# Packing the last quad's first-half operands four and five steps earlier in a four-layer attention and Fourier kernel

## The chip, the cores and the metric

The kernel runs on one core of one Trainium2 chip. The metric is the device time of one execution in microseconds (us). Three timed runs of the kernel before gave 2179.58, 2181.9 and 2183.06 us; the median is 2181.9 us. The trace comes from a fourth, profiled execution, which took 2185.11 us and whose span from the first to the last instruction is 2183.4 us. A core has five engines with an instruction queue each: PE (matrix multiply; PEld is its weight load), DVE, ACT and POOL (vector and scalar work), and SP, which in this kernel does nothing but issue DMAs, one after the other.

## The reference

Four layers alternate: sliding-window attention, Fourier mixing, attention, Fourier mixing, each on a layer-normalised input and added to it. The change touches the attention layers alone (layers 0 and 2 of the four, called the first and the second attention layer here).

```python
B, S, D = 1, 2048, 640
def _A_ref(x, wqkv, wo):
    H = 32; Dh = D // H; W = 256
    q, k, v = split_heads(x @ wqkv)              # 32 heads of 20 columns
    scores = einsum("bhqd,bhkd->bhqk", q, k) * Dh ** -0.5
    mask = (i - j >= 0) & (i - j < W)            # a window of 256 keys
    p = softmax(where(mask, scores, -1e9))
    return merge_heads(p @ v) @ wo
x = x + _A_ref(_layernorm(x), A_wqkv, A_wo)
x = x + _B_ref(_layernorm(x), ...)               # Re(DFT_seq(DFT_hidden(x)))
x = x + _A_ref(_layernorm(x), A_wqkv, A_wo)
x = x + _B_ref(_layernorm(x), ...)
```

## The kernel before

Every float32 product is made from two reduced-precision parts of each operand (three matmuls). In an attention layer the 32 heads are worked in eight quads of four heads, numbered 0 to 7, and the 2048 rows in sixteen blocks of 128. `heads` runs one loop over `step`, 16 steps to a quad. In one step it does three things for three different places of this order:

- `s_head` (L631, L636), ten steps ahead (`LEAD = 10`): the scores of one query block, only to find each row's maximum. PE multiplies `qp` by `kp`, DVE adds the mask and takes the maximum into `mc`. The first query block of a quad has 128 key columns, the second 256, the others 384. Quad 7's first block is done in step 102.
- `t_pair` and `t_exp` (L659, L669), in the step itself: the transposed scores with the maximum subtracted, which costs an extra row of `qp` (61 rows instead of 60), and the exponential on ACT, masked on POOL (L675, L679). Quad 6 is in steps 96 to 111.
- `pv` (L694, L701), one step behind: probabilities times values.

The extra row of `qp` is made by `m_rows` every fourth step: PE transposes `mc` (L644), ACT copies it to `mt` (L647), and SP stores it into `qp` with two small DMAs (L649, `qp<-mt` in the profile). The rows of quad 6's third quarter of the sequence are stored in step 98, and the first `t_pair` that reads them is that of step 102.

`kp` and `qp` are two tiles each, for even and odd quads. They are filled by `pack(quad, j)`, which loads one quarter `j` of the sequence (512 columns) from the projections that were stored in DRAM as `qk_d`. It makes twelve DMAs (L594) of 80 KB: three for each of four groups, first `kp` for the two heads pairs, then `qp`. The loop issues one group a step over four steps. When a pack begins is fixed by the list `due`: each entry holds the value of `s = step + 10` from which the pack of quad `q`, quarter `j` is made, the number of projection rounds that must be done by then, `q` and `j`. The projection matmuls (L257, `project`, `pieces`) are spread over the steps as filling between the attention matmuls; `nf` is the number of rounds for a step, the largest of a pace that ends the projection at step 96 (`ROWS_AT`) and of the paces that the entries of `due` ask for. From step 96 on the filling is instead the first part of the output projection (`partials`, also L257, and its addition on DVE, L978), whose inputs SP loads then: the residual rows (L952, 320 KB each), the attention outputs and their scales (L859, L865, 256 KB each).

All DMAs of a layer go through SP in the order of the program. The other engines' instructions are in an order of their own, fixed when the program is written out; an engine waits only where its next instruction lacks data or a free buffer.

Of the kernel before, what the change touches and what calls it, by code (L numbers as in the profile page):

```python
# [21 lines left out]
NQ = H // 4  # L22
# [8 lines left out]
AHEAD = 8  # L31
EARLY = 3
AHEAD_X = 4
AFTER = 4
ROWS_AT = 96
FIRST = 7
LATE = 9
BACK = 2
# [26 lines left out]
class Net:  # L65
# [540 lines left out]
    def heads(self, xsrc, xdst, hook):  # L606
# [98 lines left out]
        def finish(quad, bk):  # L705
# [10 lines left out]
            def store():  # L716
# [6 lines left out]
        total = NCH * NSB * per_piece  # L723
        done = [2 * NSB * per_piece]

        due = [(16 * q + 4 * j - AHEAD + 2 * (q == NQ - 1),
                ((-(-160 * (q + 1) // P) - 1) * NSB + 2 * (j // 2) + 2) * per_piece, q, j)
               for q in range(1, NQ) for j in range(NSB)]
        self.xsrc = xsrc
# [47 lines left out]
        for step in range(-LEAD, steps + 1):  # L777
# [11 lines left out]
            if due and s >= due[0][0]:  # L789
                while done[0] < due[0][1]:  # L790
                    fill(15)
                q, j = due.pop(0)[2:]
# [6 lines left out]
            if done[0] < total:  # L799
                nf = max([FIRST if t < -2 else (total - done[0]) / max(1, ROWS_AT - t)]  # L800
                         + [(d - done[0]) / max(1, at - s) for at, d, _, _ in due])
# [1064 lines left out]
```

## Time and profile before

| | us |
|---|---|
| timed runs | 2179.58, 2181.9, 2183.06 |
| median of the timed runs | 2181.9 |
| profiled execution | 2185.11 |
| its span | 2183.4 |
| PE busy in it | 2119.3 (97%) |
| DVE busy | 1602.8 (73%) |
| ACT busy | 1139.6 (52%) |
| POOL busy | 961.1 (44%) |
| DMA, mean over the span | 182 GB/s |

The profile is read as follows. A row of the timeline has the start (us from the span's start), the length in us, the engine, the line of the kernel, the operation, the tiles written and read, the shape and the number of merged instructions; in square brackets stands the idle time of the engine before the row and what ended it. "SPq" rows are issues of DMAs, and their length is the time that SP took to issue, not the transfer. The steps that the change touches lie near 412 to 446 us and 1498 to 1535 us.

### The profile page before, as it was taken

The page shows a single profiled execution, that of the slowest core. Times are in us where ns is not written, and L with a number is a line of the kernel's source. Part 1 is how long each engine was busy: PE and PEld are TensorE (multiplying, and loading weights), DVE is VectorE, ACT ScalarE, POOL GpSimd, SP SyncE. Part 2 cuts the span into 40 slices and gives each one's busy share as a digit, 9 for nine tenths or more (in the row PEclk, how much of TensorE's full clock was granted, in tenths as well). Part 3 has the DMA queues.
Part 4 walks back from the last instruction along what each step waited for, and adds up shares of the span by engine and source line. Part 5 has one row for each costly group of instructions (what it writes and reads, how often), then busy time and mean ns, then how long its engine had stood idle before and what let it go on. Part 6 is the DMA issues. An engine that isn't in the chain of part 4 may idle for free.

```text
span 2183.4 us, 48970 instructions
## 1 busy us (share of the span) xinstructions
PE 2119.3 (97%) x17872; PEld 1785.2 (82%) x17872; DVE 1602.8 (73%) x3931; ACT 1139.6 (52%) x2125; POOL 961.1 (44%) x1562
## 2 busy tenths in 40 slices
PE   8999999988999999999999999999899999999999
PEld 7987777777778888889999877776778888888899
DVE  6358888876897868786661588888768968677666
ACT  3117777756554545552441277777565645445332
POOL 3037777755513223232330377768555033231324
PEclk9999999999999999999999999999999999999999
DMA  5546666775565454655645566667845453545643
GB/s 185 174 159 193 197 189 206 214 229 178 182 197 185 133 186 135 212 194 193 209 152 182 163 188 194 193 207 216 215 155 182 142 186 126 175 157 204 220 165 125
DMA packets 227089, 398.40 MB, mean 182 GB/s; under 512 B 39969, under 2 KB 86561, under 8 KB 226849
## 3 DMA queue, kind: packets, MB, share of 16 engines
q1 hardware_dynamic: 226848, 395.28, 57.0%
q8 instruction: 141, 2.31, 0.4%
q14 instruction: 100, 0.81, 0.1%
HBM read 273.94 MB, written 120.06 MB: 180 GB/s over the span
## 4 chain that ended last, share of the span: by engine, by line
PE 79%; DVE 7%; DMA 5%; ACT 4%; issue 3%; POOL 2%; SPq 1%; ACTq 0%; DVEq 0%; POOLq 0%
PE banks L1416 29%; PE banks L239 14%; PE banks L257 13%; PE banks L694 7%; PE banks L659 6%; PE banks L631 5%; PE banks L1704 5%; DVE banks L636 1%; DMA kp<-qk_d 1%; DMA kp<-u_d 1%; DVE qp L232 1%; ACT pt L669 1%; PE banks L341 1%; ACT big L1039 1%; POOL rs L1087 1%
## 5 line engine op out<-in xcount | busy, mean ns | idle before, releaser
L636 DVE CUSTOM_DVE_ANT_0 banks<-banks,mask 128x384 f32<-128x384 f32 (+2 forms) x1024 | 527.0, 556 | 116.7 <-PE banks L631 98.9
L669 ACT ACTIVATE pt<-banks 128x768 f32<-128x768 f32 (+2 forms) x512 | 393.4, 771 | 170.7 <-PE banks L659 78.0
L675 POOL TENSOR_SCALAR_AFFINE_SELECT pt<-pt 128x256 f32<-128x256 f32 x512 | 219.0, 428 | 212.6 <-ACT pt L669 190.9
L257 PE MATMUL banks<-big,wc 64*128 64x512 f32 x1920 | 272.4, 394 | 0.4 <-DVE pt L442 0.4
L659 PE MATMUL banks<-qp,kp 61*128 61x384 f32 (+2 forms) x1024 | 210.1, 380 | 21.5 <-DVE mc L636 16.4
L694 PE MATMUL banks<-pt,vq 128*32 128x128 f32 x5760 | 211.9, 278 | 3.5 <-ACT pt L669 3.5
L631 PE MATMUL banks<-kp,qp 60*128 60x384 f32 (+2 forms) x1024 | 210.2, 350 | 4.9 <-DMA qp<-qk_d 3.5
L257 PEld LDWEIGHTS banks<-big,wc 64*128 64x128 f32 x1920 | 186.3, 185 | 23.0 <-DVE pt L442 0.5
L226 ACT ACTIVATE qp<-pt 128x512 fp32r<-128x512 f32 (+1 forms) x200 | 123.2, 625 | 129.0 <-DVE pt L1347 52.1
L679 POOL TENSOR_SCALAR_AFFINE_SELECT pt<-pt 128x256 f32<-128x256 f32 x448 | 188.3, 420 | 0.0
L232 DVE TENSOR_TENSOR qp<-pt,qp 128x512 fp32r<-128x512 f32 (+1 forms) x198 | 157.8, 805 | 40.2 <-ACT qp L226 38.6
L694 PEld LDWEIGHTS banks<-pt,vq 128*32 128x32 f32 x5760 | 142.7, 110 | 51.8 <-issue 36.3
L659 PEld LDWEIGHTS banks<-qp,kp 61*128 61x128 f32 x1024 | 108.4, 185 | 85.3 <-DVE mc L636 62.3
L1416 PE MATMUL banks<-qp,big 128*128 128x512 f32 x648 | 153.5, 390 | 0.0
L631 PEld LDWEIGHTS banks<-kp,qp 60*128 60x128 f32 x1024 | 126.7, 186 | 29.6 <-DVE mc L636 16.0
L1345 POOL TENSOR_TENSOR pt<-pt,pt 128x512 f32<-128x512 f32 x32 | 47.3, 1478 | 232.2 <-DMA pt<-c 140.3
L226 ACT ACTIVATE c<-pt 128x512 fp32r<-128x512 f32 x146 | 90.3, 625 | 109.0 <-POOL pt L1325 56.1
L636 DVE DVE_READ_ACCUMULATOR2_ANT mc<- 128x1 f32 x1024 | 143.6, 140 | 0.0
L1416 PEld LDWEIGHTS banks<-qp,big 128*128 128x128 f32 x648 | 120.7, 188 | 25.0 <-POOL qp L232 0.9
L232 DVE TENSOR_TENSOR c<-pt,c 128x512 fp32r<-128x512 f32 x144 | 113.5, 791 | 26.3 <-ACT c L226 24.0
L1416 PE MATMUL banks<-qp,xc 128*128 128x512 f32 x480 | 117.9, 393 | 3.4 <-DVE xc L232 1.9
L552 POOL CAST c<-x 128x512 fp32r<-128x512 f32 x64 | 38.8, 610 | 166.5 <-ACT x L544 162.3
(253 smaller groups left out, 4482.4 us busy)
## 6 DMA issues: line engine op xcount, KB each, us to landing
pt<-c SPq DMA_DIRECT2D x166, 512.0 KB
qk_d<-c SPq DMA_DIRECT2D x80, 512.0 KB
kp<-qk_d SPq DMA_DIRECT2D x384, 80.0 KB
qp<-qk_d SPq DMA_DIRECT2D x384, 80.0 KB
kp<-u_d SPq DMA_DIRECT2D x32, 640.0 KB
o_d<-ou SPq DMA_DIRECT2D x64, 256.0 KB
x_d<-x SPq DMA_DIRECT2D x48, 320.0 KB
v_d<-pt SPq DMA_DIRECT2D x16, 768.0 KB
```

The source lines that it names most:

```text
L226: nc.scalar.activation(hi, src, AF.Copy, scale=-1.0 if neg else 1.0)
L232: (eng or nc.vector).tensor_tensor(out=lo, in0=src, in1=hi.bitcast(F32), op=OP.subtract)
L239: self.nc.tensor.matmul(p, x, y, start=n == 0, stop=n == last)
L257: self.nc.tensor.matmul(ps[a], x[r], y[r], start=half + i == 0, stop=half == 1 and i == n - 1, skip_group_check=True)
L631: nc.tensor.matmul(p, qp[quad % 2][b:b + 60, z, qb * P:(qb + 1) * P], kp[quad % 2][b:b + 60, z, k0 * P:(qb + 1) * P], start=True, stop=True)
L636: nc.vector.tensor_tensor_reduce(out=p, in0=p, in1=self.mask[:, 384 - n * P:], scale=1.0, scalar=NEG, op0=OP.add, op1=OP.max, accum_out=mc ...
L659: nc.tensor.matmul(self.banks[:, banks[e], :n * P], kp[quad % 2][b:b + 61, z, kb * P:(kb + 1) * P], qp[quad % 2][b:b + 61, z, kb * P:(kb + ...
L669: nc.scalar.activation(pt[quad, kb][:, 2 * z:2 * z + 2, :n * P], self.banks[:, b0:b1 + 1, :n * P], AF.Exp, scale=SCALE)
L675: nc.gpsimd.affine_select(out=t[:, :, 0:P], in_=t[:, :, 0:P], pattern=[[0, 2], [1, P]], compare_op=OP.is_ge, fill=0.0, base=0, channel_mul ...
L679: nc.gpsimd.affine_select(out=t[:, :, 256:384], in_=t[:, :, 256:384], pattern=[[0, 2], [-1, P]], compare_op=OP.is_gt, fill=0.0, base=0, ch ...
L694: nc.tensor.matmul(self.banks[32 * h:32 * h + 32, bank, :P], vq[:, 96 * (kb % 4) + 21 * h:96 * (kb % 4) + 21 * h + 32], t[:, h, (qb - kb) ...
L1416: nc.tensor.matmul(self.banks[:, bk, :], p, b[q], start=start and m == 0, stop=stop and last and m == 2, skip_group_check=True)
```

## The change

The start values of the last quad's four packs become a list. For quad 7 the old expression gives `s` = 106, 110, 114, 118 for the four quarters, which is step 96, 100, 104, 108. The new list gives 102, 105, 114, 118, which is step 92, 95, 104, 108. Nothing else is changed; the number of DMAs and their contents are the same.

```diff
 ROWS_AT = 96
+LAST_DUE = (-10, -7, 2, 6)
 FIRST = 7
...
-        due = [(16 * q + 4 * j - AHEAD + 2 * (q == NQ - 1),
+        due = [(16 * q + (4 * j - AHEAD if q < NQ - 1 else LAST_DUE[j]),
                 ((-(-160 * (q + 1) // P) - 1) * NSB + 2 * (j // 2) + 2) * per_piece, q, j)
                for q in range(1, NQ) for j in range(NSB)]
```

The order of the three L594 groups by step, with the pack of quad 6's last quarter written 6.3 and so on:

| step | before | after |
|---|---|---|
| 90, 91 | 6.3 | 6.3 |
| 92, 93 | 6.3 | 6.3 and 7.0 |
| 94 | none | 7.0 |
| 95 | none | 7.0 and 7.1 |
| 96, 97, 98 | 7.0 | 7.1 |
| 99 | 7.0 | none |
| 100 to 103 | 7.1 | none |
| 104 to 111 | 7.2, 7.3 | 7.2, 7.3 |

## The prediction

> **What bounds the kernel now.** I read the page first, then PE's timeline for the end of the heads in both attention layers, then the granted clock there, then SP's timeline, since the change reorders only DMAs.
>
> ```profile
> PE 2119.3 (97%) x17872; PEld 1785.2 (82%) x17872; DVE 1602.8 (73%) x3931; ACT 1139.6 (52%) x2125; POOL 961.1 (44%) x1562
> PE 79%; DVE 7%; DMA 5%; ACT 4%; issue 3%; POOL 2%; SPq 1%; ACTq 0%; DVEq 0%; POOLq 0%
> ```
>
> PE is busy for 97% of the span and carries 79% of the chain that ended last: time lost on PE is time lost. The 5% that the chain gives to DMA is where the change can act. PE's timeline, second layer then first:
>
> ```profile
> 1499.10 0.86 PE L257 MATMUL banks<-big,wc 64*128 64x512 f32 x6
> ...
> 1506.95 0.44 PE L659 MATMUL banks<-qp,kp 61*128 61x384 f32 x2
> ...
> 1525.23 0.86 PE L694 MATMUL banks<-pt,vq 128*32 128x128 f32 x24
> 1527.24 0.45 PE L659 MATMUL banks<-qp,kp 61*128 61x384 f32 x2 [1.14 <-DMA qp<-mt]
> 1527.49 0.28 PE L631 MATMUL banks<-kp,qp 60*128 60x128 f32 x1
> 1529.66 0.32 PE L631 MATMUL banks<-kp,qp 60*128 60x128 f32 x1 [1.90 <-DMA qp<-qk_d]
> ...
> 1541.69 0.45 PE L659 MATMUL banks<-qp,kp 61*128 61x384 f32 x2 [1.40 <-DVE mc L636]
> ```
>
> ```profile
> 439.99 0.44 PE L659 MATMUL banks<-qp,kp 61*128 61x384 f32 x2 [1.22 <-DMA qp<-mt]
> ...
> 442.14 0.47 PE L631 MATMUL banks<-kp,qp 60*128 60x128 f32 x1 [1.61 <-DMA qp<-qk_d]
> ```
>
> The L631 rows with 128 columns are a quad's first query block, so this is step 102, and 1506.95 is step 96 (the first t_pair with 384 columns after quad 5's short blocks). In step 102 PE waits twice in each layer: first its L659 for the row maxima of quad 6 (`qp<-mt`, 1.22 and 1.14 us), then the second L631 for the last group of pack 7.0 (1.61 and 1.90 us). Only the second wait is for something that the change issues earlier. The clock around it:
>
> ```profile
> 442.00:445.00 3.00, 2.86 (x21) 2.86 (x23) 0.36 (x2) 0.00 (x0) 0.94 (x2) 0.50 0.78 267
> 445.00:448.00 3.00, 3.00 (x50) 2.46 (x49) 2.21 (x9) 2.21 (x5) 1.47 (x3) 0.93 0.69 213
> ...
> 1504.00:1507.00 3.00, 3.00 (x64) 2.11 (x52) 2.57 (x11) 1.92 (x7) 2.46 (x5) 1.00 0.49 160
> 1507.00:1510.00 3.00, 2.62 (x38) 1.52 (x36) 2.80 (x10) 2.35 (x6) 2.01 (x5) 1.00 0.51 128
> ...
> 1516.00:1519.00 3.00, 2.67 (x46) 2.15 (x38) 2.43 (x11) 1.56 (x5) 1.69 (x5) 1.00 1.07 270
> ...
> 1528.00:1531.00 3.00, 1.34 (x17) 1.34 (x19) 0.52 (x4) 0.59 (x1) 1.46 (x3) 0.97 0.88 268
> 1531.00:1534.00 3.00, 3.00 (x36) 2.11 (x35) 1.34 (x5) 0.90 (x2) 1.03 (x3) 0.50 0.86 208
> 1534.00:1537.00 3.00, 2.94 (x50) 2.49 (x50) 1.96 (x9) 2.35 (x5) 1.75 (x4) 0.96 0.86 212
> ```
>
> The last three columns are clock, DMA share and GB/s. Behind the waits the granted clock is 0.50 for 3 us, which costs 3 x 0.50 = 1.5 us; the edges (0.93; 0.97 and 0.96) add 0.2 us in each layer. So the pair of waits costs 1.7 us more than it shows. The DMA engines are half idle in steps 95 to 97 (0.49, 0.51) and full in step 98 to 99 (1.07). Filling that hole is what speaks for the change. What speaks against it is SP:
>
> ```profile
> 1492.18 1.19 SPq L524 DMA_DIRECT2D qk_d<-c  x1
> ...
> 1497.45 1.18 SPq L594 DMA_DIRECT2D kp<-qk_d  x3
> 1498.68 3.08 SPq L594 DMA_DIRECT2D qp<-qk_d  x3
> 1501.86 0.35 SPq L621 DMA_DIRECT2D vq<-v_d  x1
> 1502.26 1.63 SPq L594 DMA_DIRECT2D qp<-qk_d  x3
> 1503.98 0.61 SPq L711 DMA_DIRECT2D sm<-ou  x1
> 1504.64 0.48 SPq L712 DMA_DIRECT2D o_d<-ou  x1
> 1505.22 0.37 SPq L717 DMA_DIRECT2D r_d<-rc  x1
> 1505.69 1.09 SPq L649 DMA_DIRECT2D qp<-mt  x2
> 1506.84 1.19 SPq L594 DMA_DIRECT2D kp<-qk_d  x3
> 1508.13 0.35 SPq L621 DMA_DIRECT2D vq<-v_d  x1
> 1508.58 0.83 SPq L952 DMA_DIRECT2D big<-x_d  x2
> 1509.46 1.11 SPq L594 DMA_DIRECT2D kp<-qk_d  x3
> ...
> 1522.67 1.53 SPq L649 DMA_DIRECT2D qp<-mt  x2
> 1524.25 1.22 SPq L594 DMA_DIRECT2D qp<-qk_d  x3
> ```
>
> From 1497.45 to 1510.57 every row begins within 0.10 us of the end of the one before: SP is never idle there, although the DMA engines are. It has just caught up with PE when it issues step 96's group at 1506.84, beside PE's 1506.95. The first layer has the same order:
>
> ```profile
> 419.41 1.18 SPq L594 DMA_DIRECT2D kp<-qk_d  x3
> ...
> 435.06 1.43 SPq L649 DMA_DIRECT2D qp<-mt  x2
> ```
>
> **The change part by part.** *What moves.* 24 DMAs a layer. Of the eight groups, three lay ahead of step 98's `qp<-mt` (steps 96 to 98, pack 7.0); now all eight do (steps 92 to 98). The five more, 15 DMAs, go out in steps 92 to 95 between the rows above: three in each of 92, 93 and 94, six in 95. Steps 96 to 98 keep nine; steps 99 to 103 lose 15.
>
> *What the other engines do.* Nothing else moves: the pace of the projection is set by its end at step 96 and not by the entries changed. That pace, (600-d)/(96-t), stays above (570-d)/(92-t) as long as it is below 7.5 rounds a step; the fill at 1499.10 is six matmuls, three rounds. No wait is added: the last reads of those columns (quad 5's key blocks 3 and 7) are in steps 83 and 87, and the projection's store of quarter 1 is issued at 1492.18.
>
> *The price at SP.* A group of three takes from 1497.45 to 1498.68 there, 1.23 us, 0.41 each; the cheapest is 1.11/3 = 0.37, and 1502.26 has 1.63/3 = 0.54. The 3.08 us row holds waits of its own, which stay. I take 0.40, so 15 x 0.40 = 6.0 us (bounds 15 x 0.37 = 5.6 and 15 x 0.54 = 8.1; from below also 0, if something hides it). Nothing does: there is no idle SP time up to 1510.57, and from there the DMA engines are full, so that a transfer issued later lands later by as much. Step 98's `qp<-mt`, and all between, comes 6.0 us later.
>
> The Trainium skill ("DMA: Bandwidth & Descriptors", Issuing engines are not separate DMA queues) says that the time to initiate a DMA is usually small relative to the DMA itself. By it the 15 would cost their bytes only, 15 x 80 KB = 1.23 MB, which at the 270 GB/s of 1516 to 1519 is 4.6 us, less what the half-idle stretch takes up; the rows, where SP has no gap beside engines at 0.49, speak for the issue time instead.
>
> *First to be late:* the residual row for the first partial, whose DMA is the first at 1508.58. The chain of waits and DVE's timeline (second layer, then first) say when it comes and when it is needed:
>
> ```profile
> 1508.99 3.91 DMA big<-x_d
> ```
>
> ```profile
> 1515.18 0.82 DVE L978 TENSOR_TENSOR big<-banks,big 128x640 f32<-128x640 f32 x1 [0.47 <-PE banks L659]
> ```
>
> ```profile
> 427.85 0.82 DVE L978 TENSOR_TENSOR big<-banks,big 128x640 f32<-128x640 f32 x1 [0.51 <-PE banks L659]
> ```
>
> Landed at about 1508.99 + 3.91 = 1512.9, it has 2.3 us to spare; 6.0 us later it stops DVE for 3.7 us, and behind L978 on DVE stand the L636 that free PE's score banks. In the first layer I take the same.
>
> *Second:* the row maxima. Without its waits PE would begin step 102 at 1525.23 + 0.86 = 1526.1; with DVE's stop at 1529.8. The `qp<-mt` wait ended at 1527.24 and now ends at 1533.2, so the first stop is covered by the second, and the sum counts only this one. Two score matmuls follow within 0.4 us and find pack 7.0 landed long ago. So the second L631 of step 102 runs at 1533.6 instead of 1529.66: +4.0 us. In the first layer 439.99 + 6.0 + 0.4 = 446.4 instead of 442.14: +4.2 us.
>
> *The clock.* PE's idle time now comes as two stops some 10 us apart, about 3.7 and 3.4 us. A slow stretch behind the first is covered by the wait for the maxima; behind the second it costs 1.7 us as today. I count it half: -0.85 us a layer. The Trainium skill ("TensorE: Matmul & The Clock Gate", What's actually happening) has the clock halved after an idle window of about 3.4 us in a free-running grid; the 3 us at 0.50 behind some 3 us of waiting agree, and by that rule where the grid falls decides, 0 or 1.7 us a layer.
>
> *What comes back.* Steps 99 to 103 have 15 DMAs less, so SP catches up. But PE's next wait there (1541.69, 1.40 us) is for DVE's L636, no transfer; I count nothing.
>
> Sum: 4.0 + 4.2 - 2 x 0.85 = **+6.5 us**. It is made against the profiled execution (span 2183.4, 2185.11 in all, 3.2 us above the median); I expect 2191.6 there, and 2181.9 + 6.5 = **2188.4 us** as the median.
>
> **The rivals.** *The hole is filled for nothing* (faster). If the extra issues delay nothing, the waits for pack 7.0 and the slow clock go: 1.61 + 1.90 + 2 x 1.7 = 6.9 us, 2175.0; if the maxima come sooner too, another 1.22 + 1.14 = 2.4 us, 2172.6. For it: shares of 0.49 and 0.51, and SP level with PE at step 96. Against: SP level is not SP idle. It decides where `qp<-mt` is less than about 2 us later (1529.66 - 1527.24 - 0.4 = 2.0; 442.14 - 439.99 - 0.4 = 1.8).
>
> *One wait for another.* If SP makes up for some 3.5 of the 6.0 us in steps 96 to 98, the maxima come 2 to 3 us later and the sum is nearly level: 2182. For it: the SP rows between 1510.57 and 1522.67 hold waits, such as
>
> ```profile
> SPq L594 <- DMA big<-x_d: 2.4, 3, 1.1
> ```
>
> Against: these are waits for transfers in a stretch at 1.07, which come back with the load. That the change moves more or less than the twelve-DMA packs, because the planner puts other work elsewhere, would also land near here.
>
> *A heavier queue* (slower still). At 0.54 us each the shift is 8.1 us, 2.1 more in each layer: 2181.9 + 6.5 + 4.2 = 2192.6. For it: 1502.26. Against: most groups take 1.1 to 1.2 us.
>
> **How the numbers follow.** The forecast has 0.60, the heavier queue 0.10, one wait for another 0.12, the filled hole 0.18. About 0.2% (4.4 us) is what a measurement of this kernel can tell from no change. Slower by more than that: the forecast and the heavier queue, 0.69 with a little off for a covered clock; same 0.13; faster 0.18. The forecast's own range is 2184.5 (both slow stretches gone, shift 5.6) to 2192; for 8 in 10 I take 2174.5 to 2195, which reaches the filled hole at 2175.0 and leaves out its better half and a still heavier queue.
>
> **What would show it.** In the profile after: no L631 waits for `qp<-qk_d` in step 102; the `qp<-mt` wait before L659 there grows from 1.1 to some 3 us; L978 of the first partial waits for `big<-x_d`; SP issues the two L952 some 6 us later relative to PE's step 96. If instead SP shows gaps in steps 92 to 96, or the two L952 rows stay beside PE's first step of that stretch, the price at SP is wrong and the filled hole holds; if the L952 rows are late but step 98's `qp<-mt` is not, SP made up for it.

## The result and the profile after

| | before | after |
|---|---|---|
| median of six runs | 2181.7 us | 2189.68 us |
| lowest and highest | 2179.43 to 2183.06 | 2185.78 to 2190.83 |
| span of the profiled execution | 2183.4 | 2184.1 |

The change makes the kernel slower: ratio 1.0033, 95% interval 1.0022 to 1.0043, some 7.2 us (4.8 to 9.4). The profiled execution of after is the shortest of its six, so the two spans differ by 0.7 us only. ACT runs the same 2125 instructions in the same order in both; set beside each other one by one, after falls behind by 4.4 us across the changed steps of the first layer and by 2.0 us across those of the second. The 6.4 us are then largely made up where the change touches nothing: 1.3 us in the first Fourier stage, 2.8 us between 1605 and 1616 us, where only the trace of before has a slow clock (0.50 in 1610 to 1615, after 1.00), and some 2 us in the second Fourier stage. So the places are compared below relative to PE's own steps, and the size is taken from the timed runs.

The page after, busy time and chain of waits:

```profile
PE 2115.7 (97%) x17872; PEld 1784.3 (82%) x17872; DVE 1603.9 (73%) x3931; ACT 1139.8 (52%) x2125; POOL 961.2 (44%) x1562
PE 82%; DVE 7%; ACT 3%; DMA 3%; issue 2%; POOL 2%; SPq 1%; ACTq 0%; DVEq 0%; POOLq 0%
```

The totals show nothing of the loss: DMA's share of the chain even fell from 5% to 3%. One has to go to the place. (All line numbers after are one higher.) PE's timeline after, first layer and then second:

```profile
425.04 0.44 PE L660 MATMUL banks<-qp,kp 61*128 61x384 f32 x2 [0.36 <-DVE mc L637]
434.78 0.69 PE L660 MATMUL banks<-qp,kp 61*128 61x384 f32 x2 [6.41 <-DVE mc L637]
447.26 0.45 PE L660 MATMUL banks<-qp,kp 61*128 61x384 f32 x2 [1.44 <-DMA qp<-mt]
447.51 0.41 PE L632 MATMUL banks<-kp,qp 60*128 60x128 f32 x2
...
1509.61 0.45 PE L660 MATMUL banks<-qp,kp 61*128 61x384 f32 x2
1522.80 0.45 PE L660 MATMUL banks<-qp,kp 61*128 61x384 f32 x2 [3.94 <-DVE mc L637]
1535.45 0.44 PE L660 MATMUL banks<-qp,kp 61*128 61x384 f32 x2 [1.63 <-DMA qp<-mt]
1535.70 0.40 PE L632 MATMUL banks<-kp,qp 60*128 60x128 f32 x2
```

Its counterpart before in the first layer, which fixes the offset there:

```profile
425.53 0.45 PE L659 MATMUL banks<-qp,kp 61*128 61x384 f32 x2 [0.34 <-DVE mc L636]
```

Four things stand in these rows. The L632 of step 102 no longer waits for `qp<-qk_d` (they were 1.61 and 1.90 us): the change does what it says. The wait for `qp<-mt` is still there (1.44 and 1.63 us, before 1.22 and 1.14). A new stop of 6.41 and 3.94 us lies some 12 us ahead of it. And 425.04 against 425.53, 1509.61 against 1506.95 give the offsets of after to before as the stretch begins: -0.5 us in the first layer, +2.7 us in the second. DVE's timeline after says what the new stop is:

```profile
433.37 0.82 DVE L979 TENSOR_TENSOR big<-banks,big 128x640 f32<-128x640 f32 x1 [6.51 <-DMA big<-x]
1521.39 0.82 DVE L979 TENSOR_TENSOR big<-banks,big 128x640 f32<-128x640 f32 x1 [4.04 <-DMA big<-x_d]
```

DVE stands at the first partial until the residual row has landed; before, the same instruction waited 0.51 and 0.47 us, for PE. PE then waits for the L637 queued behind it. SP's timeline after, first layer and then second, and the one row of before that was not shown yet:

```profile
428.16 0.95 SPq L953 DMA_DIRECT2D big<-x  x2
...
442.73 1.55 SPq L650 DMA_DIRECT2D qp<-mt  x2
...
1510.47 1.15 SPq L595 DMA_DIRECT2D qp<-qk_d  x3
1511.80 1.09 SPq L650 DMA_DIRECT2D qp<-mt  x2
1512.93 1.27 SPq L595 DMA_DIRECT2D qp<-qk_d  x3
1514.24 2.24 SPq L595 DMA_DIRECT2D kp<-qk_d  x6
1516.58 0.35 SPq L622 DMA_DIRECT2D vq<-v_d  x1
1517.02 0.84 SPq L953 DMA_DIRECT2D big<-x_d  x2
...
1530.61 1.39 SPq L650 DMA_DIRECT2D qp<-mt  x2
```

```profile
421.13 1.49 SPq L952 DMA_DIRECT2D big<-x  x2
```

The residual rows go out at 1517.02 instead of 1508.58: 8.4 us, less the 2.7 of offset, 5.8 later. In the first layer it is 428.16 against 421.13, 7.0 + 0.5 = 7.5 later. Step 98's `qp<-mt` goes out 5.3 us later (1530.61 against 1522.67) and 8.2 later (442.73 against 435.06). The value was there long before (in the second layer ACT had written `mt` by 1519.35): it waits in SP's queue.

What holds SP there can be read from the trace's records of the single DMAs. In before and after the DMAs take eight semaphores in turn, and a DMA goes out only when the DMA eight places ahead of it in the program has landed. Of SP's gaps of more than 0.25 us in these stretches, 30 of 33 before and 25 of 31 after end within 0.1 us of such a landing. So SP's pace has two limits: the time of the issues themselves, and, where transfers land late, the landing of the eighth DMA before.

Last, the granted clock, in the windows after (busy times, then clock, DMA share and GB/s):

```profile
434.00:437.00 3.00, 2.22 (x16) 2.22 (x18) 2.38 (x9) 0.81 (x1) 0.61 (x2) 0.50 1.06 222
437.00:440.00 3.00, 3.00 (x46) 2.55 (x44) 1.32 (x6) 1.20 (x3) 0.73 (x3) 0.80 0.99 281
446.00:449.00 3.00, 1.74 (x22) 1.75 (x24) 0.81 (x6) 1.49 (x3) 1.57 (x4) 1.00 1.00 357
...
1504.00:1507.00 3.00, 3.00 (x55) 2.33 (x43) 2.68 (x11) 1.47 (x3) 2.33 (x6) 1.00 0.71 193
1507.00:1510.00 3.00, 3.00 (x54) 2.04 (x42) 2.56 (x10) 2.21 (x8) 2.57 (x6) 1.00 0.67 161
1513.00:1516.00 3.00, 2.66 (x36) 2.08 (x35) 2.55 (x11) 1.79 (x3) 3.00 (x8) 1.00 0.41 125
1525.00:1528.00 3.00, 3.00 (x42) 2.30 (x40) 1.30 (x6) 1.18 (x3) 0.77 (x2) 0.66 0.98 289
1534.00:1537.00 3.00, 1.55 (x19) 1.56 (x21) 0.81 (x6) 1.50 (x3) 1.39 (x4) 1.00 1.04 394
```

The hole is filled in part (0.71 and 0.67 where it was 0.49 and 0.51), and a new one opens behind it: 0.41 in 1513 to 1516 us, where before, at the same place of the program (1510 to 1513 us), it was 0.95: the residual rows and the rest of the queue come late. The slow stretch has moved: it lies behind the first stop (0.50 and 0.80; 0.66), ahead of the wait for the row maxima, and behind that wait the clock is 1.00.

### The profile page after: what moved, and what is told of

It reads as the page before. It is cut to its first block, busy times and chain, and to the rows that moved or that the text cites. A ratio compares the mean times of both kernels' runs of the same rounds, so it can differ in the third digit from the quotient of the medians.

```text
span 2184.1 us, 48967 instructions
## 1 busy us (share of the span) xinstructions
PE 2115.7 (97%) x17872; PEld 1784.3 (82%) x17872; DVE 1603.9 (73%) x3931; ACT 1139.8 (52%) x2125; POOL 961.2 (44%) x1562
## 4 chain that ended last, share of the span: by engine, by line
PE 82%; DVE 7%; ACT 3%; DMA 3%; issue 2%; POOL 2%; SPq 1%; ACTq 0%; DVEq 0%; POOLq 0%
PE banks L1417 29%; PE banks L240 15%; PE banks L258 13%; PE banks L695 7%; PE banks L660 6%; PE banks L1705 6%; PE banks L632 5%; DVE banks L637 1%; ACT pt L670 1%; DVE qp L233 1%; PE banks L342 1%; ACT big L1040 1%; POOL rs L1088 1%; DMA qp<-qk_d 1%; PE banks L645 1%
## 5 line engine op out<-in xcount | busy, mean ns | idle before, releaser
L637 DVE CUSTOM_DVE_ANT_0 banks<-banks,mask 128x384 f32<-128x384 f32 (+2 forms) x1024 | 527.0, 556 | 113.2 <-PE banks L632 95.1
L632 PE MATMUL banks<-kp,qp 60*128 60x384 f32 (+2 forms) x1024 | 209.1, 350 | 1.4 <-DVE mc L637 1.4
L632 PEld LDWEIGHTS banks<-kp,qp 60*128 60x128 f32 x1024 | 126.1, 186 | 25.2 <-DVE mc L637 16.0
L637 DVE DVE_READ_ACCUMULATOR2_ANT mc<- 128x1 f32 x1024 | 143.9, 140 | 0.0
```

Of the source, the lines that this page charges most:

```text
L632: nc.tensor.matmul(p, qp[quad % 2][b:b + 60, z, qb * P:(qb + 1) * P], kp[quad % 2][b:b + 60, z, k0 * P:(qb + 1) * P], start=True, stop=True)
L637: nc.vector.tensor_tensor_reduce(out=p, in0=p, in1=self.mask[:, 384 - n * P:], scale=1.0, scalar=NEG, op0=OP.add, op1=OP.max, accum_out=mc ...
```

## The experiments

Each was timed beside the kernel before on the same chip, in 5 to 12 runs; ratios are to that kernel, with 95% intervals.

**One quarter alone.** The change moves two packs; here only pack 7.0 goes early, to step 92.

```diff
-LAST_DUE = (-10, -7, 2, 6)
+LAST_DUE = (-10, -2, 2, 6)
```

> Theory (SP's queue): SP issues without a gap from step 92 on, so each DMA put ahead of step 98's qp<-mt makes it about 0.40 us later, and each ahead of the first partial's residual row delays that row. Pack 7.0 in steps 92 to 95 with pack 7.1 left at 100 to 103 puts four groups ahead of qp<-mt instead of three (3 DMAs, +1.2 us) and four instead of one ahead of the residual row (9 DMAs, +3.6 us against 2.3 us to spare, a stop of DVE of about 1.3 us that the wait for the maxima covers). The wait for pack 7.0 goes, so the second score matmul of step 102 comes 0.5 to 0.9 us earlier than in the kernel before, and the slow clock behind it may go: 1.4 to 4.8 us faster, about 2179. Rival (the early place itself): what costs is that pack 7.0 stands before step 96 and stops DVE at the residual row; then this kernel loses most of what the change loses, 2186 or more.

Measured: 2178.88 us against 2183.86, ratio 0.9974 (0.9962 to 0.9986). It is faster than both kernels. PE's timeline, then SP's in the first layer:

```profile
430.20 0.44 PE L660 MATMUL banks<-qp,kp 61*128 61x384 f32 x2 [1.83 <-DVE mc L637]
439.94 0.33 PE L632 MATMUL banks<-kp,qp 60*128 60x128 f32 x2
1523.19 0.35 PE L632 MATMUL banks<-kp,qp 60*128 60x128 f32 x2
```

```profile
425.03 1.31 SPq L953 DMA_DIRECT2D big<-x  x3
434.98 1.18 SPq L650 DMA_DIRECT2D qp<-mt  x2
```

Step 102 has no wait left, and only in the first layer a stop of 1.83 us is seen. The residual row is 4.4 us later (425.03 against 421.13, PE's rows at an offset of -0.5), but step 98's `qp<-mt` is only 0.4 us later (434.98 against 435.06); in the second layer it is 2.0 us earlier. Steps 96 to 98 now issue no pack, and SP makes up there what it lost ahead of them. So the hole is filled almost for nothing as far as pack 7.0 goes, and the loss comes with pack 7.1.

**The other quarter alone.** Pack 7.0 starts at step 96 as before, pack 7.1 at step 97.

```diff
-LAST_DUE = (-10, -7, 2, 6)
+LAST_DUE = (-6, -5, 2, 6)
```

> Pack 7.0 stays at steps 96 to 99 and pack 7.1 begins at step 97 instead of 100. Nothing is put ahead of the first partial's residual row. Theory (SP's queue): five groups instead of three stand ahead of step 98's qp<-mt, 6 DMAs or 2.4 us, and as many ahead of pack 7.0's last group, so both waits of step 102 are 2.4 us later in each layer: 4.8 us slower, about 2186.5, with no stop of DVE at the residual row. Rival (DVE's stop at the residual row is the cost, not the maxima): no change, 2181.7.

Measured: 2187.99 us against 2183.86, ratio 1.0023 (1.0014 to 1.0033). PE's timeline, second layer:

```profile
1531.47 0.69 PE L660 MATMUL banks<-qp,kp 61*128 61x384 f32 x2 [5.19 <-DMA qp<-mt]
```

With nothing taken out of steps 96 to 98 and pack 7.1 added to them, the row maxima come late without any stop ahead: PE waits 5.19 us for them here, 2.30 in the first layer. With the offsets taken off, SP issues them 2.4 us later in the first layer and 3.0 in the second, where 2.4 was expected.

**Issue time without bytes.** To the kernel before are added 15 DMAs of 512 bytes a layer, to a tile that nothing reads, where the change adds its 15.

```diff
+        self.junk, self.n_junk = dram.tile([32, 128], F32, name="junk_d"), 0
...
+            for _ in range({92: 3, 93: 3, 94: 3, 95: 6}.get(step, 0)):
+                nc.sync.dma_start(self.junk[self.n_junk:self.n_junk + 1, :], self.ones)
+                self.n_junk += 1
```

> The kernel before, with 15 added DMAs of 512 bytes each in every attention layer, three in steps 92, 93 and 94 and six in step 95, from a constant row to a scratch row of DRAM that nothing reads. Theory (SP's issue time): they cost 0.4 to 0.5 us each at SP, 6 to 8 us, although they carry almost no bytes; qp<-mt of step 98, the residual row and pack 7.0, which stays where it was, all come that much later, 6 to 8 us a layer less what a covered slow clock gives back: 2190 to 2197. Rival (bytes: the DMA engines carry the extra packs late): 15 x 512 bytes are nothing, 2182.

Measured: 2193.41 us against 2183.86, ratio 1.0048 (1.0035 to 1.0062). SP's timeline, then PE's, in the second layer:

```profile
1513.42 1.90 SPq L790 DMA_DIRECT2D junk_d<-ones  x6
1530.61 1.56 SPq L650 DMA_DIRECT2D qp<-mt  x2
```

```profile
1534.97 0.69 PE L660 MATMUL banks<-qp,kp 61*128 61x384 f32 x2 [3.79 <-DMA qp<-mt]
1537.67 0.44 PE L632 MATMUL banks<-kp,qp 60*128 60x128 f32 x1 [1.94 <-DMA qp<-qk_d]
```

Six take 1.90 us, and the 15 of a layer 4.5 us, 0.30 each. The residual row goes out 4.3 us later in the second layer and 3.1 in the first; `qp<-mt` 3.8 (1530.61 against 1522.67, at an offset of 4.1 us there) and 2.2. DMAs that move almost nothing delay the maxima by half to most of their issue time: SP's time alone costs about 0.5%, with pack 7.0's waits still in place. The Trainium skill's sentence on initiating a DMA ("DMA: Bandwidth & Descriptors", Issuing engines are not separate DMA queues), which the prediction weighed, holds here for the single DMA: in the trace of before one of a pack holds SP for 0.34 us and lands 3.6 us after its issue begins (medians of 768). But the issues of one queue add up, and a group of three holds SP for 1.1 to 1.2 us; that these times can be left out, as the prediction's reading of the sentence would have it, is contradicted by this run.

**The row maxima by another engine.** The change, with all `qp<-mt` issued by ACT.

```diff
-                self.post(1, lambda z=z: nc.sync.dma_start(
+                self.post(1, lambda z=z: nc.scalar.dma_start(
```

> The changed kernel with the qp<-mt DMAs issued by ACT, which writes mt, instead of SP; they no longer stand behind the packs in SP's order. Theory (SP's queue): the wait for qp<-mt in step 102 goes; what is left is DVE's stop at the residual row, 3.7 to 3.9 us, against the 2.8 to 3.0 us of waits and the slow clock of the kernel before: 2180 to 2185. Rival (the DMA engines are full, whoever issues): qp<-mt waits behind the bytes of the packs as before, and the kernel takes 2188 to 2190 like the changed one.

Measured: 2278.64 us against 2183.86, ratio 1.0434 (1.0421 to 1.0447), a miss. ACT's timeline:

```profile
204.39 1.08 ACTq L650 DMA_DIRECT2D qp<-mt  x2
205.60 0.66 ACT L670 ACTIVATE pt<-banks 128x256 f32<-128x256 f32 x2 [1.24 <-PE banks L632]
```

PE's timeline behind it, and a row of PE's waits over the whole run (what it waited for, us in total, times, longest):

```profile
206.03 0.44 PE L632 MATMUL banks<-kp,qp 60*128 60x384 f32 x1 [0.47 <-ACT pt L670]
```

```profile
PE banks L632 <- ACT pt L670: 38.0, 52, 1.2
```

Each issue holds ACT for 0.54 us, and the exponentials that PE waits for stand behind it. The 128 issues make 69 us; the loss is 95. PE's waits for DVE's L637 grow beside those for ACT, and the rest is not taken apart. The run says nothing of the question it was made for; a smaller version follows below.

**Issue time and bytes of the second pack.** The first experiment (pack 7.0 alone, faster) with 12 tiny DMAs added, three in each of steps 95 to 98, where the change has pack 7.1.

```diff
+            for _ in range({95: 3, 96: 3, 97: 3, 98: 3}.get(step, 0)):
```

> Pack 7.0 in steps 92 to 95 and pack 7.1 at 100 to 103, as in the run with the first quarter alone, and in the places of the changed kernel's pack 7.1 (steps 95 to 98, three each) 12 DMAs of 512 bytes to a scratch row of DRAM. SP thus issues as many DMAs ahead of step 98's qp<-mt as in the changed kernel, with 960 KB less. Issue time alone: about as slow as the changed kernel up to step 102, 2187 to 2190 at a level of 2182 before. Bytes alone: as fast as with the first quarter alone, about 0.26% faster than before. If both count, in between: a tiny DMA took 0.31 us at SP instead of 0.40, and 12 x 0.31 = 3.7 us are partly made up for while the transfers are light; I expect level with before, within 2 us.

Measured: 2186.41 us against 2184.9, ratio 1.0005 (0.9994 to 1.0016): half way from 0.9974 to 1.0033. PE's timeline and the windows, second layer:

```profile
1521.68 0.65 PE L661 MATMUL banks<-qp,kp 61*128 61x384 f32 x2 [2.71 <-DVE mc L638]
1534.76 0.45 PE L661 MATMUL banks<-qp,kp 61*128 61x384 f32 x2 [2.04 <-DMA qp<-mt]
```

```profile
1522.00:1525.00 3.00, 3.00 (x24) 3.00 (x24) 1.28 (x6) 0.81 (x1) 0.77 (x2) 0.50 0.99 312
```

The same two stops (2.76 and 0.85 us in the first layer). The clock falls behind the first, and in the second layer once more behind the second (0.73 and 0.70 in 1534 to 1540 us). SP's timeline, first layer:

```profile
428.18 0.84 SPq L957 DMA_DIRECT2D big<-x  x2
...
439.24 1.65 SPq L651 DMA_DIRECT2D qp<-mt  x2
```

With issue time alone in the place of pack 7.1 the residual rows are 6.3 and 5.9 us late (first and second layer; after: 7.5 and 5.8), and `qp<-mt` 3.5 and 3.4 us (after: 8.2 and 5.3). So the bytes of pack 7.1 add 1.2 us at most to the residual's delay; of the maxima's, they are the last 4.7 and 1.9 us. The trace shows how bytes act here: between the residual row and `qp<-mt` SP issues 20 DMAs in both kernels, but its gaps (beyond 0.05 us between two issues), in which it waits for landings, sum to 1.8 us in each layer here and to 5.0 and 4.0 after. Of the 0.59% between the first experiment and the change, 0.31% goes with the issues and 0.28% with the bytes, each uncertain by some 0.16%. The split is rough: an issue with few bytes is shorter (0.30 us against 0.37 to 0.41 us), and the tiny DMAs come on top of pack 7.1, which still goes out in steps 100 to 103.

**Where each pack starts.** Four kernels differ from the change in `LAST_DUE` alone.

> Pack 7.0 alone is moved, but only from steps 96 to 99 to steps 95 to 98. By the mere count of DMAs ahead of step 98's qp<-mt (four groups, as with the start at step 92) it should do as well as that run, 0.26% faster than before. If what helped there was that steps 96 to 98, in which the transfer engines are full, had no pack, then this kernel keeps the wait for the maxima of 1.1 to 2.4 us and loses only the wait for pack 7.0: 0 to 0.15% faster.

> Pack 7.0 alone, at steps 94 to 97: between the starts at 92 and 95. The residual row stands behind three groups instead of four, so DVE's stop there (1.8 us in the first layer with the start at 92) should go to about 0.6 us; two packs stand in steps 96 and 97. If the stop at the residual row is all that is left of the cost, this is the fastest, 0.3 to 0.35% faster than before; if the emptied steps 96 to 98 are what helps, it lies between the starts at 92 and 95.

> Pack 7.0 at steps 92 to 95 as in the change, pack 7.1 at 97 to 100 instead of 95 to 98: two of its groups instead of all four stand ahead of step 98's qp<-mt, and none ahead of the residual row. If each group ahead of the maxima costs its part, this kernel lies midway between the first quarter alone (0.26% faster) and the change (0.33% slower), level with before within 0.1%. If only the residual row counted, it would do as well as the first quarter alone.

> Pack 7.0 alone, one step earlier than in the change, steps 91 to 94; pack 7.1 at 100 to 103. The same DMAs stand ahead of the residual row and the maxima as with the start at 92, and SP has no gap in which to gain from the earlier place, so it should measure the same: 0.2 to 0.35% faster than before. If a start still earlier helps (step 95 free for SP to catch up), the stop at the residual row in the first layer, 1.8 us, goes and it is up to 0.1% faster than that.

| `LAST_DUE` | 7.0 from step | 7.1 from step | us against before | ratio | waits for `qp<-mt` in step 102, us |
|---|---|---|---|---|---|
| (-7, -2, 2, 6) | 95 | 100 | 2182.32, 2184.9 | 0.9991 (0.9978 to 1.0003) | 3.02, 1.27 |
| (-8, -2, 2, 6) | 94 | 100 | 2180.93, 2184.9 | 0.9981 (0.9969 to 0.9993) | 1.89, 0.53 |
| first experiment | 92 | 100 | 2178.88, 2183.86 | 0.9974 (0.9962 to 0.9986) | none |
| (-11, -2, 2, 6) | 91 | 100 | 2179.25, 2184.47 | 0.9976 (0.9966 to 0.9986) | none |
| (-10, -5, 2, 6) | 92 | 97 | 2187.43, 2184.47 | 1.0013 (1.0001 to 1.0024) | 2.62, 4.12 |
| the change | 92 | 95 | 2189.68, 2181.7 | 1.0033 (1.0022 to 1.0043) | 1.44, 1.63 |

The wait for the row maxima falls as pack 7.0 leaves steps 96 to 98, and is gone with a start at step 92. A step earlier brings nothing more: a wait for the maxima of the quarter before, 0.64 and 0.63 us in step 98, comes in its place. Pack 7.1 put into those steps loses it all again, and more the earlier it starts; with the start at 97, expected level within 0.1%, the kernel is 0.13% slower. The wait itself is not the measure: with pack 7.1 from step 95 the stop ahead of it, at the residual row, is 6.41 and 3.94 us and covers part of it, with pack 7.1 from 97 it is 2.39 and 0.94.

**One late transfer taken out of the queue.** The last three kernels are the change with the first residual row, with step 98's `qp<-mt`, or with both issued by ACT: one, two and three DMAs a layer.

```diff
-                self.nc.sync.dma_start(self.y_part(t), self.xsrc[t * P:(t + 1) * P, :])
+                (self.nc.sync if t else self.nc.scalar).dma_start(
+                    self.y_part(t), self.xsrc[t * P:(t + 1) * P, :])
```

```diff
-                self.post(1, lambda z=z: nc.sync.dma_start(
+                self.post(1, lambda z=z: (nc.scalar if (quad, u) == (6, 2) else nc.sync).dma_start(
```

> The change with one DMA a layer, the residual row for the first partial, issued by ACT instead of SP. Theory of the forecast (the first stop is covered by the second): the stop at the residual row (PE idle 3.94 and 6.41 us) falls below 1 us, PE reaches step 102 that much earlier and waits there for qp<-mt 5 to 8 us instead of 1.63 and 1.44; the wait ends within 0.5 us of where it ended, and the slow clock behind it is no longer covered (up to +1.7 us a layer). Time from level with the change to 0.15% slower: ratio 1.0025 to 1.005. Rival, the two stops add up: 10 us come back, ratio 0.998 to 1.000, with waits for qp<-mt as before.

> The change with two DMAs a layer, the qp<-mt of step 98 alone, issued by ACT instead of SP. Both theories: no wait for qp<-mt in step 102, the stop at the residual row stays at some 4 and 6.5 us. Forecast: 1.63 + 1.44 us come back, less two issues of 0.54 us a layer on ACT where they lie on PE's path (0 to 2.2 us), less the slow clock, which is then uncovered (0 to 3.4 us): ratio 1.0015 to 1.0045. Rival, the row maxima alone carry the loss: the whole 7.3 us come back, ratio 0.999 to 1.001.

> The change with both edits: the first residual row and step 98's qp<-mt issued by ACT, three DMAs a layer. Theory (these two late transfers carry the whole loss): neither stop is there, no slow clock in the heads, and the time is that of the change of the first quarter alone plus at most 3 issues x 0.54 us x 2 layers = 3.2 us: ratio 0.997 to 0.9995, which would also show the loss to lie in the order of the queue and not in the bytes. Rival, the next transfer in the queue is late in their place (a group of the packs or the second residual row): PE waits 2 us or more at another row in steps 96 to 102, ratio 1.001 or more.

Against 2184.0 us before, the maxima alone gave 2188.3, ratio 1.0026 (1.0015 to 1.0036). PE's timeline:

```profile
428.37 0.45 PE L660 MATMUL banks<-qp,kp 61*128 61x384 f32 x2 [0.36 <-DVE mc L637]
436.73 0.69 PE L660 MATMUL banks<-qp,kp 61*128 61x384 f32 x2 [5.04 <-DVE mc L637]
448.23 0.23 PE L632 MATMUL banks<-kp,qp 60*128 60x128 f32 x2
...
1511.66 0.45 PE L660 MATMUL banks<-qp,kp 61*128 61x384 f32 x2
1525.52 0.69 PE L660 MATMUL banks<-qp,kp 61*128 61x384 f32 x2 [4.58 <-DVE mc L637]
1537.04 0.23 PE L632 MATMUL banks<-kp,qp 60*128 60x128 f32 x2
```

The wait for the maxima is gone; the stop at the residual row stays, and most of the loss with it. From the first row of each layer to step 102's L632 it takes 448.23 - 428.37 = 19.86 and 1537.04 - 1511.66 = 25.38 us, in the change 22.47 and 26.09: 2.6 and 0.7 us come back. The two waits were 1.44 and 1.63, and the first stop is 1.4 us shorter in the first layer and 0.6 longer in the second; that makes 2.8 and 1.0. So taking the second wait away returns no more than what is seen of it (the ratios of the two kernels, 1.0026 and 1.0033, do not differ beyond their intervals), and the rival that the maxima alone carry the loss (0.999 to 1.001) falls.

With the residual row moved the result was a miss: 2203.54, ratio 1.0092 (1.0079 to 1.0106), and with both 2194.9, ratio 1.0050 (1.0037 to 1.0062). SP's waits between 1510 and 1535 us, with the residual row moved, and the row of SP's timeline (waiting engine and line, what it waited for, us in total, times, longest):

```profile
SPq L595 <- DMA big<-x_d: 6.0, 1, 6.0
```

```profile
1515.00 7.00 SPq L595 DMA_DIRECT2D qp<-qk_d  x3
```

SP itself now stood 6.0 us in a pack's group until the residual row that ACT had issued was there (5.6 in the first layer; 5.4 and 6.3 with both edits), and everything behind it came late. The records of the single DMAs show why. The turn of eight semaphores goes by the program's order, whichever engine issues: ACT's DMA had one of them, and the next DMA that uses it is SP's, in this group. SP was ready for it at 1515.36, ACT issued its own only at 1518.47, it landed at 1521.33, and SP went on at 1521.34. In the run with the maxima moved SP is held in the same way (2.6 and 3.2 us behind the first residual row). A DMA handed to ACT is out of SP's queue but not out of the turn. So whether the first stop alone, taken away, would leave the second to grow in its place was tried and not answered.

## Why the prediction was right

It forecast 2188.4 us, slower by 6.5; the runs give 2189.68, slower by 7.2 (4.8 to 9.4). By its own steps:

- **The price at SP.** 15 x 0.40 = 6.0 us, at the residual rows and at step 98's `qp<-mt`. Measured 5.8 and 5.3 us in the second layer, 7.5 and 8.2 in the first. For the residual rows it is nearly all issue time, as argued (tiny DMAs in the place of pack 7.1 do nearly the same): from step 90's `qp<-mt` to the residual row SP issues 36 DMAs instead of 21, which without the gaps takes 5.9 us more in the first layer and 6.4 in the second. But "SP is never idle there" was read from merged rows: inside the row of 3.08 us SP stood 0.61 and 1.59 us until an earlier DMA had landed. Such gaps do not stay as they were, as the prediction had it; up to the residual row they grow from 1.8 to 3.2 us in the first layer and shrink from 2.4 to 1.2 in the second, and that is most of what sets the layers apart. For `qp<-mt` the sum was right for another reason: there "nothing hides it" is too simple. The first experiment has three DMAs more ahead of `qp<-mt` than before, which at 0.40 is 1.2 us, and measured +0.4 and -2.0, because packs taken out of the full steps 96 to 98 give time back there; the change fills these steps again with pack 7.1.
- **First to be late, the residual row.** Predicted 3.7 us of DVE in both layers; 4.04 in the second and 6.51 in the first. The first layer was taken like the second, and was not: there the row went out 7.5 us late and then took 5.1 us to land (428.16 to 433.28, by the last update of its semaphore) instead of 4.4 (421.13 to 425.50). In the second layer the time to spare before was 1.9 us and not 2.3: the row of the chain from which 1512.9 was worked out begins at the second residual row's issue, and the first landed at 1513.28.
- **Second, the row maxima, and one stop covering the other.** The second L632 of step 102 was to come 4.0 and 4.2 us later. With the offsets taken off, 1535.70 is 6.0 later than 1529.66, less 2.7, that is 3.4; 447.51 against 442.14 is 5.4 + 0.5 = 5.9. The wait was forecast at some 3 us and was 1.63 and 1.44, because the first stop, much longer in the first layer, and the slow stretch behind it take up the rest. That the stops do not add up is read from SP's timeline: between the residual row and `qp<-mt` all its gaps of more than 0.25 us but one (0.42 us) end at a landing and not at a step of PE, so the maxima would have come about as late without the first stop. The runs do not settle it: without the second wait only its visible length came back, which would be so either way, and the run without the first stop did not answer.
- **The clock.** Counted half, 0.85 us a layer; the slow stretch lies behind the first stop in both layers and the clock behind the maxima's wait is 1.00, so the whole 1.7 is saved in each. The Trainium skill's rule of a free-running grid ("TensorE: Matmul & The Clock Gate", What's actually happening) left 0 or 1.7 us open; both layers took the same side here. The trace of after agrees with the grid: its first four slow stretches begin at 431.36, 642.99, 1523.62 and 1684.05 us, 62, 258 and 47 times 3.413 us apart, and last 3.41 or 6.83 us. The sum with these sizes is 3.4 + 5.9 - 3.4 = 5.9 us, inside the interval. The L632 came 1.1 us later in all than forecast and the clock gave back 1.7 us more, so that the total is this close is in part luck. That the slow stretch is covered is read from the trace; no run took it away alone.
- **What comes back later.** None was counted. The wait for DVE's L636 in step 105, 1.40 us, is still there at 1.40.
- **The rivals.** A filled hole, 2175.0, is what pack 7.0 alone does (ratio 0.9974, some 5.7 us faster): right for half of the change, and the forecast did not see that its two packs differ in sign. One wait for another, 2182, fails on `qp<-mt`, for which SP made up nothing. The heavier queue, 2192.6, has the delay of the first layer (8.2 us / 15 = 0.55 each at the maxima), not of the second, and not its cause: the issues take 0.40 and 0.43 us each, and the rest is SP's waiting for landings.

## What to carry to other kernels

A DMA moved into a stretch where the DMA engines are half idle is free only if the issuing queue has gaps there too, or if as much leaves a later full stretch before the next urgent transfer. List what is queued behind the moved issues, with the time each has to spare (here a residual row with some 2 us and 4 KB of row maxima), and move only so many that these still go out in time or nearly so: half of this change gains 0.26%, the whole loses 0.33%. Look inside a merged row of issues, too: a gap in it can be a wait for an earlier DMA to land, and it does not keep its length when the order changes. A DMA given to another engine leaves the queue, but here it kept its place in the turn of eight semaphores. Two waits in a row on one engine can count as the later end and not as their sum, so look at both before removing one.

## What was not expected of the hardware

- A DMA of 512 bytes holds SP for 0.30 us, one of 80 KB for some 0.4.
- A DMA of the row maxima holds ACT for 0.54 us (1.08 for two), as long as it holds SP (1.09 for two); the kernel with 128 of them on ACT was 95 us slower. A residual row of 320 KB held ACT for 0.33 to 0.40 us.
- The DMAs of this program take eight semaphores in turn over all issuing engines, so one that is late on ACT held SP for 5.4 to 6.3 us.
- The clock fell to 0.50 after a single stop of 2.71 us (the tiny DMAs in the place of pack 7.1), as it did before after two waits of 1.14 and 1.90 us; a stop of 1.83 us (the first experiment, with a mean granted clock of 0.999) left it up, while one of 1.89 us (pack 7.0 from step 94, 0.58 in 443 to 446 us) did not. So the length of the stop alone does not decide.
